# Attention and two expert layers on one core: column sums in two columns, a guard column for the combine sums, and a new plan of all queues

## The chip, the cores and the metric

The kernel runs on one core of one Trainium2 chip. The metric is the time of one execution on the device in microseconds (us); lower is better. The engines are PE (TensorE, matmuls), DVE (VectorE), ACT (ScalarE), POOL (GpSimd) and SP, which here only issues DMA transfers. Each engine works its own list of instructions in order and waits on semaphores for the others.

## What is computed

Three layers in a row. Blockwise causal attention over 8 batches, 8 heads, 576 positions of width 64; its output, 4608 rows of 512, goes through a soft mixture of experts (32 slots, 8 experts), and that through a bilinear layer.

```python
# attention, for each batch and head (blocks of 64 positions)
scores = scale * q @ k.T                     # masked where block_i < block_j
attn = exp(scores - max(scores, axis=-1))
attn = attn / (sum(attn, axis=-1) + 1e-09)
x = attn @ v
# soft mixture of experts on x (4608 x 512)
logits = x @ phi                             # 4608 x 32
d = exp(logits - logits.max(0)); d /= d.sum(0) + 1e-09     # dispatch: over all rows
slot_in = d.T @ x                            # 32 x 512, 4 slots per expert
slot_out[e] = relu(slot_in[e] @ w1[e]) @ w2[e]
c = exp(logits - logits.max(1)); c /= c.sum(1) + 1e-09     # combine: over 32 slots
x = c @ slot_out
# bilinear layer
out = ((x @ w1) * (x @ w2)) @ w3 @ w_out
```

## The kernel before

**Stages.** The attention stage takes the 64 heads as 32 pairs (n = 0 to 31), four pairs to a batch. Behind it come a short tail with the last batch's dispatch (`push_tail`), the experts together with the preparation of the weights of the last layer (`Rest.run`), and the output (`Rest.final`).

**One pair.** The steps have short names, which are those of the planner and of the methods `op_...`: `ld` and `ldv` load the pair (SP); `cast` (ACT, line 310) and `sub` (POOL, line 317) split it in a high and a low part; `M0` to `M3` (PE, line 329) make coarse scores, and `R0` to `R3` (DVE, line 333) reduce them to maxima in tile `bm`; `l2`, `mT`, `mc` and `mx` join the maxima, transpose them, copy them out and write them by four small transfers (lines 355 and 356, `shift<-mT`) into the tile X, from which the exact score matmuls `Q0` to `Q3` (PE, line 369) subtract them; `E0` to `E3` (ACT, line 377) are the exponentials, `P0`, `P1`, `P3` (POOL, line 387) sums of them, `V1` and `V0` (PE, lines 402 and 406) the products with v, `SU` (PE, line 418) and `sb` (DVE) the row sums. Scores of `M` and `Q` share three buffers in PSUM: a `Q` can start only when a reduction or an exponential has freed one.

**One batch**, while the next pairs run: `r` takes the reciprocals of the row sums (DVE, line 444), `rw` writes them to memory and `rd` reads them back spread over the partitions (SP, lines 449, 450 and 455), `sx0` to `sx3` multiply by them (POOL, line 459), `lg` makes the logits (PE, line 468) and `lgT` transposes them. The combine weights: `cm` maxima (line 487), `csub` (POOL, line 491), `cexp`, `csm` (DVE: sum in line 498, `+ 1e-9` in line 499, reciprocal in line 500), `cmul` (POOL, line 504), `cT` and its write. The dispatch weights: `LTm` (running column maxima, DVE), `LTe` (ACT, lines 544 to 548: two exponentials with their sums in `dac`, and `dal`, the factor by which older sums shrink when the maximum grows), `Ls` (DVE, lines 555 and 556: running column sums, the second part with weight 0.25, since the last 64 rows of a batch are held four times), `dn`, `xn0` to `xn4`, `S` and `SSu` (slot inputs).

**Fillers.** `b`-steps turn 64-bit weights of the last layer into f32 (a load and DVE and ACT steps, lines 823 to 838); `win` (line 848) loads the first expert windows, 2 MB each.

**What sets the order.** In the attention stage every engine's list is written out by the class `Plan`: each step has an engine, a guessed duration, a guessed time to landing (`lat`) for transfers, the steps it comes after, and a due time, n x PERIOD + OFF (plus EARLY for the first four pairs; for a batch step 4 x (batch + 1) x PERIOD + OFF). PE's list is the steps sorted by due time alone. The other engines take, at each moment of the planner's own clock, of the steps that become ready within LOOK the one with the least due time plus WAIT for each us it would have to be waited for. The planner's times only make the order; on the chip each engine goes by semaphores.

## Time and profile before

| | |
|---|---|
| three timed runs | 649.78, 649.06, 641.72 us; median 649.06 |
| profiled execution | 648.8 us, its span 647.0 us |
| granted PE clock over the span | 0.952 of full speed |
| PE busy | 597.0 us (92%) |
| PE weight loads | 433.3 us (67%) |
| DVE busy | 429.9 us (66%) |
| ACT busy | 323.1 us (50%) |
| POOL busy | 336.4 us (52%) |

The span runs from the first to the last instruction of the profiled execution; the device time has a little around it. PE's busy time is no measure of how dense its work is, since matmuls overlap in its pipeline; its idle time before an instruction, with what ended it, is the more telling figure. Granted clock 1.00 is 2.4 GHz and 0.50 is 1.2 GHz.

### The profile page before, as it was taken

How to read it: one execution, taken by the hardware profiler on the slowest of the kernel's cores; microseconds unless marked ns; L12 is line 12 of the kernel's file. 1: busy time of each engine (PE TensorE's matmuls, PEld its weight loads, DVE VectorE, ACT ScalarE, POOL GpSimd, SP SyncE). 2: the span in 40 equal slices, each digit the busy share in tenths (PEclk: the TensorE clock that was granted, in tenths of full speed). 3: DMA queues.
4: the chain of work that ended last, by engine and by line, in shares of the span. 5: the costliest groups of instructions: out<-in, count | busy, mean ns of one | idle time of the engine just before them, and what ended most of it. 6: DMA issues, size and time to landing. Idle time of an engine off the chain costs nothing.

```text
span 647.0 us, 13943 instructions
## 1 busy us (share of the span) xinstructions
PE 597.0 (92%) x5487; PEld 433.3 (67%) x5487; DVE 429.9 (66%) x714; ACT 323.1 (50%) x618; POOL 336.4 (52%) x245
## 2 busy tenths in 40 slices
PE   7999699989899899899897978879999979999997
PEld 4777577777676676677775745336655757888886
DVE  5568377786786786777782457899626998545550
ACT  4666277556564664665552622454324345444541
POOL 6879468858758578588464400344225223222220
PEclk8999699989989999999797997989999988999999
DMA  6356725526348239246145398999780314565642
GB/s 198 125 168 228 233 83 127 167 91 163 123 127 204 82 102 231 77 117 190 54 104 208 112 398 326 391 423 381 273 332 19 116 46 143 190 207 198 224 153 97
DMA packets 40441, 116.96 MB, mean 181 GB/s; under 512 B 6572, under 2 KB 16796, under 8 KB 38312
## 3 DMA queue, kind: packets, MB, share of 16 engines
q1 hardware_dynamic: 40196, 116.00, 54.0%
q8 instruction: 43, 0.70, 0.4%
q14 instruction: 22, 0.18, 0.1%
q10 hardware_dynamic: 180, 0.07, 0.0%
HBM read 105.75 MB, written 10.45 MB: 180 GB/s over the span
## 4 chain that ended last, share of the span: by engine, by line
PE 70%; DVE 12%; DMA 8%; issue 4%; ACT 3%; POOL 2%; SPq 0%; ACTq 0%; DVEq 0%; POOLq 0%
PE sc L369 16%; PE ops L1211 16%; PE pv L402 10%; PE wps L907 6%; PE sc L329 5%; DVE bm L333 4%; DMA shift<-mT 3%; PE pv L418 3%; DVE csm L499 2%; PE h L987 2%; DMA raw<-in_moe_w 2%; PE pv L468 1%; PE so L1014 1%; POOL wo L853 1%; PE ops L1213 1%
## 5 line engine op out<-in xcount | busy, mean ns | idle before, releaser
L333 DVE TENSOR_REDUCE bm<-sc 128x10 f32<-128x640 f32 (+2 forms) x128 | 122.6, 985 | 37.2 <-PE sc L329 36.8
L369 PE MATMUL sc<-set 64*128 64x320 f32 (+4 forms) x1152 | 124.3, 324 | 10.7 <-DVE bm L333 9.8
L369 PEld LDWEIGHTS sc<-set 64*128 64x128 f32 x1152 | 97.0, 201 | 22.8 <-DVE bm L333 14.2
L1211 PE MATMUL ops<-H,Ph 128*128 128x512 f32 x288 | 92.7, 402 | 3.0 <-ACT H L1115 2.5
L317 POOL TENSOR_TENSOR set<-raw,set 128x1152 fp32r<-128x1152 f32 x32 | 84.7, 2648 | 5.6 <-ACT set L310 2.4
L387 POOL TENSOR_TENSOR acc<-PTa,PTb 128x640 f32<-128x640 f32 x32 | 49.8, 1556 | 53.1 <-PE pv L418 44.8
L369 PE MATMUL sc<-shift 64*128 64x320 f32 (+4 forms) x384 | 64.5, 318 | 10.5 <-DMA shift<-mT 10.5
L1186 POOL TENSOR_TENSOR Pl<-rot,Ph 128x384 fp32r<-128x384 f32 x24 | 28.5, 1207 | 80.1 <-ACT Ph L1184 80.1
L1211 PEld LDWEIGHTS ops<-H,Ph 128*128 128x128 f32 x288 | 55.6, 193 | 17.3 <-ACT H L1115 2.9
L1211 PE MATMUL ops<-H,Pl 128*128 128x512 f32 x144 | 57.9, 402 | 0.0
L377 ACT ACTIVATE PTa<-sc 128x1024 f32<-128x1024 f32 x32 | 32.8, 1026 | 42.4 <-PE sc L369 37.9
L907 PE MATMUL wps<-wo,w 128*128 128x512 f32 x192 | 50.5, 405 | 2.7 <-POOL wo L853 1.7
L329 PE MATMUL sc<-set 64*128 64x320 f32 (+4 forms) x384 | 50.7, 338 | 0.8 <-ACT set L313 0.5
L369 PEld LDWEIGHTS sc<-shift 64*128 64x128 f32 x384 | 42.1, 202 | 13.3 <-DMA shift<-mT 12.8
L1214 ACT COPY o<-ops 128x512 f32<-128x512 f32 x36 | 21.1, 587 | 59.4 <-PE ops L1213 59.1
L387 POOL TENSOR_TENSOR acc<-acc,PTc 128x640 f32<-128x640 f32 x31 | 48.1, 1553 | 2.4
L907 PEld LDWEIGHTS wps<-wo,w 128*128 128x128 f32 x192 | 34.3, 188 | 20.1 <-issue 5.8
L411 ACT COPY xT<-pv 128x256 f32<-128x256 f32 (+1 forms) x64 | 25.5, 398 | 42.4 <-PE pv L406 32.0
L402 PE MATMUL pv<-PTc,v 128*64 128x256 f32 (+1 forms) x256 | 44.9, 430 | 1.0 <-ACT xT L411 1.0
L377 ACT ACTIVATE PTb<-sc 128x1024 f32<-128x1024 f32 x32 | 32.8, 1026 | 25.1 <-PE sc L369 23.4
L459 POOL TENSOR_TENSOR xT<-xT,shift 128x576 f32<-128x576 f32 x28 | 38.7, 1418 | 6.0 <-DMA shift<-rr 5.9
L377 ACT ACTIVATE PTc<-sc 128x640 f32<-128x640 f32 (+1 forms) x64 | 39.3, 650 | 3.7 <-PE sc L369 3.3
(246 smaller groups left out, 1161.7 us busy)
## 6 DMA issues: line engine op xcount, KB each, us to landing
win<-in_moe_w SPq DMA_DIRECT2D x16, 2048.0 KB
raw<-in_qk SPq DMA_DIRECT2D x32, 576.0 KB
v<-in_v SPq DMA_DIRECT2D x32, 320.0 KB
...
```

The costliest lines, as they stand in the source:

```text
L317: self.nc.gpsimd.tensor_tensor(lo, self.raw.pop(n), hi.bitcast(F32), op=ALU.subtract)
L329: self.nc.tensor.matmul(ps[:, h, o:o + kn], lhsT=qh[r, q0:q0 + 128], rhs=kh[r, k0:k0 + kn], start=True, stop=True)
L333: self.nc.vector.tensor_reduce(self.bmb[n % 2][:, :, o:o + m // 64], self.st.pop(("M", n, i))[:, :, 0:m].rearrange("p h (n k) -> p h n k", ...
L369: self.nc.tensor.matmul(ps[:, h, o0:o0 + w], lhsT=lt[r, k] if i < 3 else lt[r], rhs=rt[r, q0:q0 + w], start=i == 0, stop=i == 3)
L377: self.nc.scalar.activation(out=out, in_=ps[:, :, 0:sum(g[3] for g in self.UNITS[u])], func=AF.Exp, scale=SCALE)
L387: eng.tensor_tensor(acc[:, :, lo:hi], a, b, op=ALU.add)
L402: mm(ps[64 * h:64 * h + 64, q0 - lo:q1 - lo], lhsT=v[:, 128 * j + 64 * h:128 * j + 64 * h + 64], rhs=pt[:, h, o:o + q1 - q0], start=j == 0 ...
L411: self.nc.scalar.copy(self.xTb[b % 2][:, p, lo:hi], self.st.pop(("V", n, part))[:, 0:hi - lo])
L459: self.nc.gpsimd.tensor_tensor(x, x, self.rb[:, i], op=ALU.mult)
L907: nc.tensor.matmul(p, lhsT=a[:, o], rhs=b, start=c + i == 0, stop=c == 7 and i == 2)
L1186: eng.tensor_tensor(Pl[:, k], p, Ph[:, k].bitcast(F32), op=ALU.subtract)
L1211: nc.tensor.matmul(ps, lhsT=a[:, k, r], rhs=b[:, k], start=n == 0, stop=False)
```

## The change

Four things are edited. The column sums `Ls` are kept as two columns, one for each part: ACT multiplies the old ones by `dal` into a second row of `dac` (a new instruction of the first stage's `LTe`), one tensor_reduce on DVE adds the two rows, and the weight 0.25 is applied once, in the tail (`slot_sum`). The combine tile becomes a fixed tile of 33 columns, whose last column holds 1e-9, so that the reduction of line 498 adds the guard and line 499 goes; `cmul` now writes to a tile of its own. The planner's guesses change: 4.5 for 2.5 us to the landing of `rw`, 1.2 for 0.9 for `rd`, 0.52 for 0.9 for `csm`, and a little for `LTm`, `LTe` and `Ls`. The first window may be loaded after `Q0` of pair 6 instead of pair 4, and all due times and weights of the planner are other numbers.

```diff
--- before.py
+++ after.py
@@ -49,21 +49,21 @@
         nc.tensor.matmul(ps[:, 0:w], lhsT=keep["zeros"][:, 0:128], rhs=keep["zeros"][:, 0:w], start=True, stop=True)
 
 
-OFF = dict(ld=(145.85, -848.37, -88.58, 261.17), ldv=(773.65, 351.15, 347.6, 182.58),
-           cast=(-181.02, 301.68, 319.14, 419.66), sub=(278.96, -1281.51, 354.57, 216.03),
-           M0=(-68.45, -54.13, -78.59, -81.82), M1=(-72.52, -78.33, -71.42, -71.5),
-           M2=(-55.98, -86.85, -79.57, -63.38), M3=(-81.49, -85.42, -53.82, -73.3),
-           l2=(290.43, -440.49, -293.73, 999.35), mT=(-49.53, -43.88, -30.18, -33.86),
-           Q0=(-5.78, -20.61, -12.45, -4.41), Q1=(-2.38, -12.38, -4.76, 1.02), Q2=(1.6, -11.32, 8.14, 2.98),
-           Q3=(2.1, -9.94, 8.7, 1.71), P0=(-95.26, -384.06, -174.37, 299.52), P3=(104.53, 57.2, 67.07, 87.61),
-           V1=(42.63, 10.62, 11.84, 43.54), V0=(38.28, 27.09, 45.61, 18.15), SU=(23.27, 42.91, 38.78, 30.39),
-           r=254.78, sx0=162.82, sx1=-63.54, sx2=347.2, sx3=-32.45, lg=76.82, lgT=95.84, cm=652.17, cT=197.25,
-           LTm=16.4, dn=93.94, xn0=128.66, xn1=124.74, xn2=86.67, xn3=140.4, xn4=85.48, S=156, b=38.53)
-EARLY = dict(M=(-238.5, -160.13, -145.3, 8.44), m=(-163.57, -156.29, -130.1, 1.33), Q=(-156.25, -148.89, -5.6, -8.96))
-PERIOD = 32.899
-LOOK = dict(DVE=31.59, ACT=44.54, POOL=172.62, SP=79.34, PE=0)
-WAIT = dict(DVE=296.04, ACT=1322.25, POOL=154.39, SP=284.92, PE=0)
-BG0, BGS = 51.196, 1.727
+OFF = dict(ld=(192.13, -1003.31, 33.96, 308.08), ldv=(831.02, 395.8, 343.91, 147.85),
+           cast=(-124.13, 280.4, 312.63, 559.84), sub=(331.24, -1528.88, 431.86, 185.24),
+           M0=(-92.56, -65.33, -85.04, -97.01), M1=(-83.11, -82.9, -64.5, -69.87),
+           M2=(-58.52, -95.12, -80.33, -69.5), M3=(-92.88, -103.93, -50.22, -77.92),
+           l2=(332.47, -478.49, -253.38, 1132.37), mT=(-45.31, -39.92, -30.94, -41.28),
+           Q0=(-4.59, -16.6, -20.99, -9.6), Q1=(1.74, -11.46, -15.55, -5.94), Q2=(9.94, -9.79, -10.49, 6.36),
+           Q3=(-0.56, 0.89, 1.37, -2.61), P0=(37.42, -380.68, -165.87, 339.59), P3=(78.95, -43.79, 66.52, 137.55),
+           V1=(46.45, 9.48, 15.55, 44.48), V0=(39.73, 18.63, 52.08, 19.86), SU=(28.42, 39.49, 34.94, 34.16),
+           r=357.46, sx0=107.5, sx1=-193.83, sx2=217.14, sx3=11.51, lg=77.98, lgT=88.4, cm=705.09, cT=211.89,
+           LTm=13.08, dn=96.18, xn0=140.54, xn1=136.25, xn2=83.74, xn3=140.69, xn4=94.04, S=174.13, b=97.56)
+EARLY = dict(M=(-296.49, -199.51, -176.61, 5.24), m=(-238.54, -183.36, -167.65, -7.99), Q=(-174.47, -175.48, 3.44, -3.46))
+PERIOD = 35.238
+LOOK = dict(DVE=49.08, ACT=63.74, POOL=172.99, SP=85.93, PE=0)
+WAIT = dict(DVE=183.79, ACT=1358.44, POOL=120.38, SP=490.54, PE=0)
+BG0, BGS = 46.084, 1.836
 MX = ((.35, 1.22), (.29, 1.1), (.21, .83), (.24, .83))
 QK = ((1.2, 1.03), (1.11, 1.03), (.68, .71), (.54, .6))
 SHAPE = {"rows": .06, "cols": .08, "quarters": .28, "full": .07}
@@ -119,8 +119,8 @@
             at = lambda *names: [(x, b) for x in names]
             last = NP_B * b + NP_B - 1
             op("r", "DVE", 2.2, [("sb", last)] + old(b - 1, "rw"))
-            op("rw", "SP", 1.9, at("r") + old(b - 2, "rd"), lat=2.5, due="r", late=.1)
-            op("rd", "SP", .9, at("rw") + old(b - 1, *quarter("sx")), lat=8., due="r", late=.2)
+            op("rw", "SP", 1.9, at("r") + old(b - 2, "rd"), lat=4.5, due="r", late=.1)
+            op("rd", "SP", 1.2, at("rw") + old(b - 1, *quarter("sx")), lat=8., due="r", late=.2)
             for i in range(4):
                 op(f"sx{i}", "POOL", 1.45, at("rd") + [("c1", last - 3 + i), ("c0", last - 3 + i)])
             op("lg", "PE", 1.34, at(*quarter("sx")) + old(b - 1, "lgT", "LTe"), "pv", mode="quarters")
@@ -130,14 +130,14 @@
             op("cm", "DVE", .32, at("L4"))
             op("csub", "POOL", .46, at("cm") + old(b - 1, "cT"), due="cm", late=.1)
             op("cexp", "ACT", .34, at("csub"), due="cm", late=.2)
-            op("csm", "DVE", .9, at("cexp"), due="cm", late=.3)
+            op("csm", "DVE", .52, at("cexp"), due="cm", late=.3)
             op("cmul", "POOL", .46, at("csm"), due="cm", late=.4)
             op("cT", "PE", .32, at("cmul") + old(b - 1, "cTd"), "pv")
             op("cTc", "ACT", .46, at("cT"), free="cT", due="cT")
             op("cTd", "SP", 1.2, at("cTc"), lat=3, due="cT")
-            op("LTm", "DVE", .6, at("lgc"))
-            op("LTe", "ACT", 1., at("LTm") + old(b - 1, "dn", "SSu", "Ls"), due="LTm", late=.1)
-            op("Ls", "DVE", .3, at("LTe"), due="LTm", late=.2)
+            op("LTm", "DVE", .68, at("lgc"))
+            op("LTe", "ACT", 1.2, at("LTm") + old(b - 1, "dn", "SSu", "Ls"), due="LTm", late=.1)
+            op("Ls", "DVE", .16, at("LTe"), due="LTm", late=.2)
             op("dn", "PE", .3, at("LTe") + old(b - 1, "S"), "pv")
             op("dnc", "ACT", .35, at("dn"), free="dn", due="dn")
             for c in range(5):
@@ -156,7 +156,7 @@
             op("bm", "ACT", .67, at("bl") + old(j - 1, "b4"), due="b")
             op("b4", "DVE", .7, at("b3"), free="b1", due="b", late=.3)
         self.due = lambda t: t * PERIOD
-        for i, (t, after) in enumerate(((20, [("Q0", 4)]), (N - 3, [(q, n) for n in (N - 4, N - 3) for q in quarter("Q")]),
+        for i, (t, after) in enumerate(((20, [("Q0", 6)]), (N - 3, [(q, n) for n in (N - 4, N - 3) for q in quarter("Q")]),
                                         (N - 1, [(q, n) for n in (N - 2, N - 1) for q in quarter("Q")]),
                                         (N - 1, [(q, N - 1) for q in quarter("Q")]))):
             self.op(("win", i), "SP", .45, after, lat=10, due=t)
@@ -261,6 +261,7 @@
         self.xTb = [p.tile([128, NP_B, SP], F32, name=f"xT{i}") for i, p in enumerate((self.x_p, self.const))]
         self.Sb = self.const.tile([128, 384], F32, name="Sb")
         self.Lg = self.const.tile([128, 2, SP], F32, name="Lg")
+        self.C = self.const.tile([128, 5, 33], F32, name="Cb")
         self.dT = self.const.tile([128, 256], F32, name="dT")
         self.stage = self.xTb[1].rearrange("p a b -> p (a b)")
         self.xconst = self.stage[:, 640:640 + S]
@@ -271,6 +272,7 @@
         nc.vector.memset(self.ones, 0.0)
         for p in range(NP_B):
             nc.vector.memset(self.ones[:, p, p:p + 1], 1.0)
+        nc.gpsimd.memset(self.C[:, :, 32:33], EPS)
         nc.gpsimd.memset(self.Sb, 0.0)
         nc.gpsimd.memset(self.L[64:128, 4], 0.0)
         nc.gpsimd.memset(self.Lg[:, :, S:SP], 0.0)
@@ -487,21 +489,19 @@
         self.nc.vector.tensor_reduce(mx, self.L, axis=AX.X, op=ALU.max)
 
     def op_csub(self, b, _):
-        C = self.st["C"] = self.tl([128, 5, 32], "c")
-        self.nc.gpsimd.tensor_tensor(C, self.L, self.st["cm"].unsqueeze(2).to_broadcast([128, 5, 32]), op=ALU.subtract)
+        self.nc.gpsimd.tensor_tensor(self.C[:, :, 0:32], self.L, self.st["cm"].unsqueeze(2).to_broadcast([128, 5, 32]), op=ALU.subtract)
 
     def op_cexp(self, b, _):
-        self.nc.scalar.activation(out=self.st["C"], in_=self.st["C"], func=AF.Exp)
+        self.nc.scalar.activation(out=self.C[:, :, 0:32], in_=self.C[:, :, 0:32], func=AF.Exp)
 
     def op_csm(self, b, _):
         sm = self.st["csm"] = self.tl([128, 5], "csm")
-        self.nc.vector.tensor_reduce(sm, self.st["C"], axis=AX.X, op=ALU.add)
-        self.nc.vector.tensor_scalar(sm, sm, EPS, None, op0=ALU.add)
+        self.nc.vector.tensor_reduce(sm, self.C, axis=AX.X, op=ALU.add)
         self.nc.vector.reciprocal(sm, sm)
 
     def op_cmul(self, b, _):
-        C = self.st["C"]
-        self.nc.gpsimd.tensor_tensor(C, C, self.st["csm"].unsqueeze(2).to_broadcast([128, 5, 32]), op=ALU.mult)
+        C = self.st["C"] = self.tl([128, 5, 32], "c")
+        self.nc.gpsimd.tensor_tensor(C, self.C[:, :, 0:32], self.st["csm"].unsqueeze(2).to_broadcast([128, 5, 32]), op=ALU.mult)
 
     def op_cT(self, b, slot):
         ps, C = self.pv_b[slot], self.st["C"]
@@ -540,20 +540,18 @@
         self.nc.vector.tensor_scalar(ng, M, -1.0, None, op0=ALU.mult)
 
     def exps(self, b, t):
-        ac, ng, act = self.tl([128, 2], "dac"), self.st["ng"], self.nc.scalar.activation
-        act(out=self.dT[:, 0:128], in_=t[:, 0:128], func=AF.Exp, bias=ng, accum_out=ac[:, 0:1])
-        act(out=self.dT[:, 128:192], in_=t[:, 128:192], func=AF.Exp, bias=ng, accum_out=ac[:, 1:2])
+        ac, ng, act = self.tl([128, 2, 2], "dac"), self.st["ng"], self.nc.scalar.activation
+        act(out=self.dT[:, 0:128], in_=t[:, 0:128], func=AF.Exp, bias=ng, accum_out=ac[:, 0, 0:1])
+        act(out=self.dT[:, 128:192], in_=t[:, 128:192], func=AF.Exp, bias=ng, accum_out=ac[:, 0, 1:2])
         if b:
             al = self.st["al"] = self.tl([128, 1], "dal")
             act(out=al, in_=self.keep["M"][b % 2][:, 2:3], func=AF.Exp, bias=ng)
+            self.nc.scalar.mul(ac[:, 1], self.keep["Ls"], al)
         self.st["ac"] = ac
 
     def sums(self, b):
-        Ls, ac = self.keep["Ls"], self.st["ac"]
-        add = self.nc.vector.scalar_tensor_tensor
-        if b:
-            add(Ls, Ls, self.st["al"], ac[:, 0:1], op0=ALU.mult, op1=ALU.add)
-        add(Ls, ac[:, 1:2], 0.25, Ls if b else ac[:, 0:1], op0=ALU.mult, op1=ALU.add)
+        ac = self.st["ac"][:, 0:2 if b else 1]
+        self.nc.vector.tensor_reduce(self.keep["Ls"], ac.rearrange("p k c -> p c k"), axis=AX.X, op=ALU.add)
 
     def op_LTm(self, b, _):
         self.maxima(b, self.st["lgc"])
@@ -715,7 +713,9 @@
 
         def slot_sum():
             ps = pst("ML")
-            for i, t in enumerate((self.keep["M"][1 - b % 2][:, 2:3], self.keep["Ls"])):
+            Ls, tot = self.keep["Ls"], tl([128, 1], "tot")
+            nc.vector.scalar_tensor_tensor(tot, Ls[:, 1:2], 0.25, Ls[:, 0:1], op0=ALU.mult, op1=ALU.add)
+            for i, t in enumerate((self.keep["M"][1 - b % 2][:, 2:3], tot)):
                 nc.tensor.transpose(ps[0:1, 128 * i:128 * i + 128], t, ident)
             by_slot = lambda t: t.rearrange("p (g s) -> p s g", g=4)
             rows = lambda t: t.unsqueeze(1).to_broadcast([1, 4, 32])
@@ -1234,7 +1234,7 @@
     keep["sel32"] = kp.tile([128, 32], F32, name="sel32")
     keep["zeros"] = kp.tile([128, 512], mybir.dt.bfloat16, name="zeros")
     keep["M"] = [kp.tile([128, 3], F32, name=f"M{i}") for i in range(2)]
-    keep["Ls"] = kp.tile([128, 1], F32, name="Ls")
+    keep["Ls"] = kp.tile([128, 2], F32, name="Ls")
     keep["SS"] = kp.tile([128, 512], F32, name="SS")
     keep["L"], keep["C"] = (kp.tile([128, 5, 32], F32, name=f"last_{n}") for n in "LC")
     keep["siT"] = kp.tile([128, 4, 32], F32, name="siT")
```

## Rows read from the trace of the kernel before

**Rows 1.** Busy time by stretch: start:end, length, PE PEld DVE ACT POOL, PEclk

```profile
0.00:377.00 377.00, 350.04 (x4142) 262.17 (x4142) 257.15 (x440) 214.53 (x392) 263.09 (x184) 0.95 0.49 148
```

**Rows 2.** Waits: engine, line, waited for: us in total, times, longest

```profile
PEld sc L369 <- DVE bm L333: 14.2, 15, 2.2
...
PE sc L369 <- DMA shift<-mT: 10.5, 4, 5.3
...
PE sc L369 <- DVE bm L333: 9.8, 6, 2.0
```

**Rows 3.** Timeline of DVE: start us, us, line, operation [idle before <-what ended it]

```profile
219.43 0.75 DVE L555 SCALAR_TENSOR_TENSOR Ls<-Ls,dal,dac 128x1 f32<-128x1 f32 x1 [1.14 <-ACT dal L548]
220.21 2.55 DVE L556 SCALAR_TENSOR_TENSOR Ls<-dac,Ls 128x1 f32<-128x1 f32 x1
222.79 1.55 DVE L333 TENSOR_REDUCE bm<-sc 128x10 f32<-128x640 f32 x2
...
232.80 0.31 DVE L498 TENSOR_REDUCE csm<-c 128x5 f32<-128x160 f32 x1
233.14 2.41 DVE L499 TENSOR_SCALAR csm<-csm 128x5 f32<-128x5 f32 x1
...
237.37 2.15 DVE L444 RECIPROCAL rS<-Sb 128x320 f32<-128x320 f32 x1
```

**Rows 4.** Timeline of POOL, same batch and the next pairs

```profile
232.87 2.65 POOL L317 TENSOR_TENSOR set<-raw,set 128x1152 fp32r<-128x1152 f32 x1
...
237.26 1.56 POOL L387 TENSOR_TENSOR acc<-PTa,PTb 128x640 f32<-128x640 f32 x1 [0.88 <-ACT PTb L377]
...
252.79 5.52 POOL L459 TENSOR_TENSOR xT<-xT,shift 128x576 f32<-128x576 f32 x4 [0.74 <-DMA shift<-rr]
```

**Rows 5.** Timeline of PE, same batch

```profile
223.67 0.88 PE L369 MATMUL sc<-set 64*128 64x448 f32 x6 [1.97 <-DVE bm L333]
...
231.22 0.60 PE L527 MATMUL pv<-ident,xT 128*128 128x128 f32 x4
231.75 0.86 PE L369 MATMUL sc<-set 64*128 64x448 f32 x6
...
254.11 0.93 PE L369 MATMUL sc<-shift 64*128 64x448 f32 x2 [0.84 <-DMA shift<-mT]
...
260.41 1.50 PE L468 MATMUL pv<-xT,phi 128*32 128x128 f32 x64
```

**Rows 6.** Single lines: least/median/longest ns, first and last start us

```profile
L499 DVE TENSOR_SCALAR csm<-csm x7: 172/2416/2433, 98.5 to 372.9; 128x5 f32<-128x5 f32 x7
...
L556 DVE SCALAR_TENSOR_TENSOR Ls<-dac,Ls x7: 159/2549/2550, 128.9 to 391.3; 128x1 f32<-128x1 f32 x7
...
L548 ACT ACTIVATE dal<-M,dng x7: 278/279/289, 127.8 to 390.2; 128x1 f32<-128x1 f32 x7
```

**Rows 7.** Chain that ended last, in order of time: start us, us, what

```profile
188.22 2.43 DVE csm L499
...
277.91 2.41 DVE csm L499
...
324.16 2.44 DVE csm L499
```

**Rows 8.** Busy time by stretch again, two stretches of low PEclk (columns as in group 1)

```profile
72.40:83.10 10.70, 10.69 (x79) 8.31 (x83) 6.36 (x8) 5.80 (x9) 3.55 (x3) 0.50 0.39 144
...
311.80:318.60 6.80, 6.80 (x50) 6.06 (x50) 4.41 (x7) 2.78 (x5) 0.46 (x1) 0.50 0.25 80
```

**Rows 9.** Timeline of SP, transfers issued: start us, us of issue, line, operation

```profile
52.83 0.43 SPq L848 DMA_DIRECT2D win<-in_moe_w  x1
...
61.47 1.42 SPq L455 DMA_DIRECT2D shift<-rr  x2
...
241.41 1.40 SPq L455 DMA_DIRECT2D shift<-rr  x2
...
247.61 0.66 SPq L355 DMA_DIRECT2D shift<-mT  x1
```

## Prediction

> **What bounds the kernel now.** Five views were read, from coarse to fine. The stretches by stage come first: the attention stage is 377 of the 647.0 us of the span, and in it PE is busy 350.0, DVE 257.2, ACT 214.5 and POOL 263.1 us [rows 1]. PE runs one list in a fixed order, so a microsecond in which PE stands there is a microsecond of the end, and a microsecond of another engine counts only where PE ends up waiting for it. The diff touches this stage and a few instructions of the tail, so the question is where PE stands in it. The waits say: 9.8 us on the row maxima (line 333) and 10.5 us on the transfer that writes the maxima into X, `shift<-mT` [rows 2]. PE's timeline shows the first kind as a wait of 1.97 us at 223.67 [rows 5]; it comes back once in each of five batches, at 132.35, 177.23, 223.67, 268.44 and 311.63 (one row stands for the five; the sum of the five is nearly all of the 9.8).
>
> The maxima are only the messenger. On DVE the reduction that PE wants starts at 222.79, straight behind line 556, which takes 2.55 us for one column [rows 3]. Its median over seven is 2549 ns and its least 159 ns [rows 6]: the same instruction takes a sixteenth of that when nothing holds it. Line 499 is its twin: 2.41 us for five columns from 233.14, least 172 ns, and it ends at 235.55, when POOL's `sub` of 2.65 us that began at 232.87 ends too [rows 3, 4, 6]. So a DVE instruction with two operands in SBUF (556), or this form of tensor_scalar (499), waits for the POOL instruction that began before it. A tensor_reduce doesn't: line 498 took its 0.31 us from 232.80, across the start of that `sub` [rows 3, 4].
>
> **The change part by part.** Profiled execution: 648.8 us, span 647.0, so 1.8 us lie around it; the median of three is 649.06, and the sum is made against 648.8.
>
> *A, column sums.* Lines 555 and 556 go; one ACT multiplication and one tensor_reduce over four numbers come. In the list as it is, DVE gets ACT's last result at 219.43 and starts the wanted reduction at 222.79 [rows 3]. After: the multiplication costs what line 548, also one small ACT instruction, costs, 279 ns [rows 6], and the reduction at most the 0.31 us of line 498, which reads 160 columns. The wanted reduction then starts at 219.43 + 0.28 + 0.31 = 220.0, 2.8 us sooner; the wait that goes with it is 1.97. It goes wholly, with 0.8 us to spare, even if the list were not changed. Five times: **-9.7**. ACT's added 0.28 us lie inside DVE's wait and are in this reckoning; ACT is busy only 214.5 of 377 [rows 1]. The first batch's sums and those of the tail never stood on PE's path for long; the tail gains one DVE instruction for the final 0.25 weight and one on ACT: **+0.3**.
>
> *B, guard as a column.* Line 499 goes, seven times, six of them held. The reductions behind it start 2.4 us sooner, but PE had other work there: of 15 weight loads that waited for maxima, 14.2 us, five of at most 2.2 are those of A, so the other ten share at least 3.2 [rows 2]. Six of them follow a held 499; I take **-1.5**, bounds 0 and -3.2. The reduction over 33 columns for 32, the memset of the column and the separate output of `cmul` add instructions of a shape that is there already, on engines that are idle a third of the time: nothing, or 0.1 us a batch if POOL reads a pitch of 33 more slowly.
>
> Does the reciprocal of line 500 take over the wait of 499? The row that bears on it: line 444's reciprocal began at 237.37, 0.11 us after a POOL instruction of 1.56 us, and took 2.15 us, its time everywhere [rows 3, 4]. It was not held, so nothing moves. The Trainium skill (VectorE: DVE Perf Modes, What auto-detection actually checks) goes by operands: one source and a destination in SBUF of equal dimensions let an instruction take the second port, and line 500 is of that kind. By it 500 would be held as 499 was and B would give nothing, 631.5; the trace's row speaks against it, and the rule keeps a small chance below.
>
> *C, PE's clock.* After some of the waits of A the granted clock stood at 0.50 (1.2 GHz): 6.8 us from 311.8 [rows 8], and two like stretches of 3.4 us, from 134.3 and from 178.7 (one row stands for the three); none after the waits at 223.67 and 268.44. From one line 499 to the next is a batch: 188.22 to 233.14 is 44.92 us at full clock, and less its waits of 1.97 and, at 209.35, about 1.0 (like the 0.84 at 254.11) it is 41.9; 277.91 to 324.16 is 46.25, less 1.97 is 44.3, so 6.8 us of half clock cost 2.4, 0.35 a microsecond [rows 3, 5, 7]. For 13.6 us in all: **-4.4** (bounds 0 and -6.8, half of it all).
>
> *D, the first window.* The planner now lets the 2 MB load `win` go after pair 6 instead of pair 4. Before, it went at 52.83 in front of the writes of the reciprocals; the read behind these could go only at 61.47, 8.6 us later, straight into the transfers for pair 6 [rows 9]. This is the longest wait of PE for X, 5.3 us [rows 2], and it was followed by 10.7 us at half clock [rows 8], 3.7 by C's price: 9.0. In steady batches the read goes early enough (241.41, with the maxima of the pair at 247.61) that only 0.84 us are left at 254.11 [rows 5, 9]. The load is late next: it now stands somewhere ahead of pair 7's maxima and delays them if these come within its 8.6 us. I keep 2.5 for that: **-6.5**, bounds 0 and -9.0.
>
> *E, the new lists.* PE's list is its steps sorted by due time, so it can be worked out from the diff. Example: before, dn of batch 3 is due at 16 x 32.899 + 93.94 = 620.3, Q0 of pair 19 at 19 x 32.899 - 4.41 = 620.7, lgT at 622.2; after, lgT at 652.2, mT of pair 20 at 659.5, Q0 at 659.9, dn at 660.0. So lgT and the transposes move ahead of Q0 and dn behind it: more work of PE stands in front of the place of A. Ahead of Q0 of pairs 2, 6, 10 ... (the 0.84 us at 254.11) stands M0 of a later pair, 0.3 us more cover. The sorted list has 242 changes of the array's mode where it had 231. Four transposes from 231.22 take 0.60 us, 0.11 apart, and the first row-mode matmul follows the last of them by 0.20, at 231.75 [rows 5]: 0.09 for a change, **+1.0**. The lists of the other queues depend on the planner's clock and can't be read off. In it the writes of the reciprocals now last 2.0 us longer, so the read may be listed behind a load of the next pair. Waits that I can't place: **+2.0**, bounds 0 and, if each of seven batches got one more like the 0.84, +6.
>
> Sum: -9.7 + 0.3 - 1.5 - 4.4 - 6.5 + 1.0 + 2.0 = -18.8; 648.8 - 18.8 = **630.0 us**. All stages behind attention start from its end and move with it.
>
> **The rivals.** *The window load collides again* (with pair 7 as before with pair 6): D gives 0 and its reserve falls away, 636.5. For it: 2 MB are 2 MB; against it: the reciprocals' writes no longer queue behind it. *The read goes late*: SP lists it behind the next pair's load, it lands about 2 us later in each of seven batches and PE waits for X at the place of 254.11; with half clock behind some waits that is 2.4 a batch, +17, 647. For it: the planner's 4.5; against it: without 499 the reciprocals start up to 2.4 us sooner, which makes up for it. *Slower*: SP lists the read behind the maxima of the pair, past 250 instead of at 241.41 [rows 9], 8.7 us later. POOL's four multiplications by it ran from 252.79 for 5.5 us, to 258.3, and PE's list came to `lg`, which needs them, at 260.41 [rows 4, 5]. So from 2.1 us of delay on PE stands. The read would then find the queues emptier, so I count 4 of the remaining 6.6 us, in seven batches, and 1 each by the clock: +35, 665. Against it: a planner that reckons 8 us for the read sees this wait. *The reciprocal is held in place of 499*: line 500 starts where 499 did, in the first half microsecond of POOL's `sub`, waits for its end [rows 3, 4], and the 1.5 of B stay, 631.5; against it stands line 444, as said.
>
> **How the numbers follow.** Chances: forecast 0.57 (own range 622 to 637: C, D and E at their bounds), window again 0.15, late read 0.15, slower 0.08, reciprocal held 0.05. Time: 630.0. Range 620 to 648: below lies only C and D both in full, above it the slower rival and a part of the late read, together under 0.2. About 2%, 13 us, is what a measurement of this kernel can tell from no change. Faster by more, under 636.1: 0.52 of the forecast's 0.57, 0.07 of the window's, 0.04 of the last, 0.63. Slower by over 2%: 0.09. Within: 0.28.
>
> **What would show it.** A: no wait of PE near 2 us for line 333 in the batches; the sums' instruction on DVE at most 0.31 us long while POOL works. B: the reciprocal of the combine sums at its 0.19 us right behind the reduction, with POOL's `sub` still running. C: no half clock inside the batches between 90 and 330. D: no wait of 5 us for `shift<-mT` around 72, and batches of about 42 us from the first on. E: waits for `shift<-mT` of at most 1 us. The prediction is wrong if the batches stay near 45 us with the waits of A gone: then PE stands for X or for `lg` instead, and the read of the reciprocals on SP's timeline says which.

## The result, and the profile after

The changed kernel takes 621.42 us (median of 4 runs, 619.46 to 622.58) against 647.33 us; the ratio is 0.9608 with a 95% interval of 0.9536 to 0.9681, so it is faster by about 26 us. Timed again in a later comparison it gave 620.98 us and 0.9631 [0.9566, 0.9696]. The prediction was 630.0 us with a range of 620 to 648. The profiled execution is 620.63 us with a span of 618.8 us, 28.2 less than the span of before where the sum said 18.8 less.

In the code after, the names are the old ones and the lines move by two or so: the scores are lines 331 and 371, the row maxima 335, the reduction of the combine sums 499, its reciprocal 500, the column sums 554, POOL's `sub` 319 and `acc` 389.

The attention stage, busy time by stretch (length, PE, PEld, DVE, ACT, POOL, PEclk, DMA share, GB/s), which answers [rows 1]:

```profile
0.00:352.00 352.00, 336.86 (x4130) 253.51 (x4130) 225.08 (x426) 213.85 (x398) 262.40 (x185) 0.99 0.53 158
```

The stage ends 25 us sooner. DVE gives back 32 us of busy time, nearly all of it held time and not work: in the kernel before, the held runs of lines 499, 555 and 556 took some 29 us more than at their least. The granted clock rose from 0.95 to 0.99. PE's waits up to 345 us (us in total, times, longest), to set against [rows 2]:

```profile
PE sc L371 <- DMA shift<-mT: 3.0, 4, 1.6
PE pv L404 <- ACT xT L413: 2.0, 3, 1.1
...
PE sc L371 <- DVE bm L335: 0.9, 3, 0.3
```

The 9.8 us for the row maxima are 0.9, and the 10.5 us for the transfer into X are 3.0. The combine sums of a batch, to set against line 499 and POOL's `sub` in [rows 3, 4], in timelines of DVE and POOL of the kernel after:

```profile
218.13 0.32 DVE L499 TENSOR_REDUCE csm<-Cb 128x5 f32<-128x165 f32 x1
218.48 0.19 DVE L500 RECIPROCAL csm<-csm 128x5 f32<-128x5 f32 x1
218.73 1.96 DVE L335 TENSOR_REDUCE bm<-sc 128x16 f32<-128x1024 f32 x2
```

```profile
217.67 1.55 POOL L389 TENSOR_TENSOR acc<-acc,PTc 128x640 f32<-128x640 f32 x1 [0.28 <-ACT PTc L379]
```

The reduction and the reciprocal both ran inside a POOL instruction that began before them, neither was held, and the maxima follow 0.6 us after these sums began. In six of the seven places the two ran inside such an instruction and took their usual time; in the seventh POOL was idle. The column sums are short too, seven of their eight runs inside a POOL instruction (single line: least/median/longest ns):

```profile
L554 DVE TENSOR_REDUCE Ls<-dac x8: 146/146/158, 81.0 to 364.3; 128x2 f32<-128x4 f32 x7, 128x2 f32<-128x2 f32 x1
```

SP's transfers around the first window, to set against [rows 9]:

```profile
57.24 1.41 SPq L457 DMA_DIRECT2D shift<-rr  x2
62.74 0.68 SPq L357 DMA_DIRECT2D shift<-mT  x1
...
68.74 0.44 SPq L848 DMA_DIRECT2D win<-in_moe_w  x1
```

The read of the reciprocals (`shift<-rr`) goes 4 us sooner, and the window goes behind the maxima (`shift<-mT`) of its pair.

**A table for all kernels below.** All kernels but before and after are the runs of the next section. A batch is four pairs, and its length is read from ACT's timeline as the time between the first exponentials of two pairs that lie four apart. "Start" runs up to the first of them at pair 5, "five batches" are those after the first one, "last" runs from the last such mark to the end of the last exponential, "rest" from there to the end. Half clock is the time at 0.50 that begins between 90 and 320 us, where only the steady batches are. All in us, one profiled execution each.

| kernel | ratio to before, 95% | start | first batch | five batches | last | rest | half clock |
|---|---|---|---|---|---|---|---|
| before | 1 | 57.0 | 50.4 | 226.0 | 34.2 | 279.4 | 13.6 |
| after | 0.9608 [0.9536, 0.9681] | 58.4 | 42.8 | 210.8 | 30.8 | 275.9 | 0 |
| after, again | 0.9631 [0.9566, 0.9696] | 59.3 | 42.7 | 211.2 | 31.2 | 276.0 | 6.8 |
| edits alone | 0.9649 [0.9612, 0.9686] | 56.2 | 47.7 | 206.4 | 34.5 | 275.9 | 0 |
| plan alone | 0.9835 [0.9786, 0.9883] | 59.1 | 43.5 | 229.4 | 33.7 | 276.6 | 20.4 |
| column sums alone | 0.9758 [0.9706, 0.9810] | 57.0 | 48.5 | 212.0 | 35.4 | 276.2 | 0 |
| guard alone | 0.9957 [0.9923, 0.9991] | 57.0 | 48.0 | 223.5 | 35.6 | 278.5 | 17.0 |
| before, window late | 0.9949 [0.9909, 0.9989] | 56.2 | 43.7 | 228.2 | 34.5 | 278.7 | 17.0 |
| after, window early | 0.9678 [0.9619, 0.9736] | 59.8 | 47.2 | 208.5 | 31.4 | 276.7 | 0 |
| before, filled | 0.9853 [0.9799, 0.9906] | 56.3 | 47.8 | 216.4 | 36.1 | 277.2 | 0 |
| after, second window | 0.9610 [0.9559, 0.9662] | 59.3 | 42.7 | 206.7 | 27.5 | 275.3 | 0 |
| after, both tuned | 0.9524 [0.9482, 0.9566] | 59.1 | 43.1 | 207.5 | 27.3 | 274.0 | 0 |
| after, filler's square late | 0.9585 [0.9535, 0.9636] | 59.8 | 43.1 | 209.6 | 32.8 | 275.7 | 0 |
| edits, windows moved | 0.9481 [0.9427, 0.9535] | 56.9 | 45.4 | 205.2 | 29.7 | 278.5 | 0 |

Before against after, by column: +1.4, -7.6, -15.2, -3.4, -3.5, together -28.2 (with rounding). The profiled executions of "plan alone" (644.1 us) and of "edits, windows moved" (617.5) were the slowest of their runs and those of "filled" and of "second window" the fastest, so their rows count more for which waits stand in them than for their sums. The last but one column runs from 274.0 to 279.4 for kernels whose code there hardly differs, and it largely goes with the time at half clock behind the attention stage: 13.7 us in the kernel with 274.0, 20.5 in the kernel after, 24.6 in the kernel before, which has the largest value of all. By the price of experiment 4 these 4.1 us are 1.9 of the -3.5. No run takes the rest apart; I take it for the spread of single executions and not for the change.

The first batch has such a spread too. The filled kernel runs the same instructions as the kernel before until its first zeros, behind this batch, and its first batch is 47.8 us, not 50.4: the kernel before had 13.7 us of half clock behind its wait at the first window, the filled one 6.8 behind the same wait. So about 2.6 of the -7.6 are a longer half clock in the one profiled execution of before and no work of the change.

### The profile page after: what moved, and what is told of

Read it like the earlier page. It is cut to its first block, busy times and chain, and to the rows that moved or that the text cites. A ratio compares the mean times of both kernels' runs of the same rounds, so it can differ in the third digit from the quotient of the medians.

```text
span 618.8 us, 13858 instructions
## 1 busy us (share of the span) xinstructions
PE 581.2 (94%) x5475; PEld 423.2 (68%) x5475; DVE 396.7 (64%) x701; ACT 322.6 (52%) x625; POOL 337.8 (55%) x246
## 4 chain that ended last, share of the span: by engine, by line
PE 70%; DMA 13%; DVE 9%; POOL 3%; issue 3%; ACT 2%; SPq 0%; POOLq 0%; DVEq 0%; ACTq 0%
PE ops L1211 16%; PE sc L371 15%; PE pv L404 9%; DMA raw<-in_moe_w 7%; PE wps L907 7%; PE sc L331 4%; PE pv L420 4%; PE pv L527 3%; PE so L1014 2%; DVE bm L335 2%; DMA w3raw<-in_w3T 2%; PE h L987 2%; DMA raw<-in_qk 1%; PE ops L1213 1%; PE pv L470 1%
## 5 line engine op out<-in xcount | busy, mean ns | idle before, releaser
L371 PE MATMUL sc<-set 64*128 64x320 f32 (+4 forms) x1152 | 118.9, 313 | 1.5 <-DVE bm L335 0.9
L371 PEld LDWEIGHTS sc<-set 64*128 64x128 f32 x1152 | 92.3, 190 | 13.3 <-issue 6.3
L389 POOL TENSOR_TENSOR acc<-PTa,PTb 128x640 f32<-128x640 f32 x32 | 49.8, 1556 | 64.3 <-PE pv L420 43.5
L1186 POOL TENSOR_TENSOR Pl<-rot,Ph 128x384 fp32r<-128x384 f32 x24 | 30.6, 1296 | 76.8 <-ACT Ph L1184 76.8
L371 PE MATMUL sc<-shift 64*128 64x320 f32 (+4 forms) x384 | 61.6, 306 | 3.0 <-DMA shift<-mT 3.0
L379 ACT ACTIVATE PTc<-sc 128x512 f32<-128x512 f32 (+1 forms) x64 | 41.4, 649 | 24.2 <-PE sc L371 24.0
L907 PE MATMUL wps<-wo,w 128*128 128x512 f32 x192 | 50.4, 406 | 1.9 <-POOL wo L853 1.3
L331 PE MATMUL sc<-set 64*128 64x320 f32 (+4 forms) x384 | 48.2, 330 | 2.8 <-ACT set L312 1.9
L907 PEld LDWEIGHTS wps<-wo,w 128*128 128x128 f32 x192 | 34.5, 189 | 19.0 <-issue 5.4
L371 PEld LDWEIGHTS sc<-shift 64*128 64x128 f32 x384 | 39.2, 190 | 5.9 <-DMA shift<-mT 5.3
L379 ACT ACTIVATE PTb<-sc 128x1024 f32<-128x1024 f32 x32 | 32.8, 1026 | 17.1 <-PE sc L371 13.5
```

Of the source, the lines that this page charges most:

```text
L331: self.nc.tensor.matmul(ps[:, h, o:o + kn], lhsT=qh[r, q0:q0 + 128], rhs=kh[r, k0:k0 + kn], start=True, stop=True)
L371: self.nc.tensor.matmul(ps[:, h, o0:o0 + w], lhsT=lt[r, k] if i < 3 else lt[r], rhs=rt[r, q0:q0 + w], start=i == 0, stop=i == 3)
L379: self.nc.scalar.activation(out=out, in_=ps[:, :, 0:sum(g[3] for g in self.UNITS[u])], func=AF.Exp, scale=SCALE)
L389: eng.tensor_tensor(acc[:, :, lo:hi], a, b, op=ALU.add)
L907: nc.tensor.matmul(p, lhsT=a[:, o], rhs=b, start=c + i == 0, stop=c == 7 and i == 2)
L1186: eng.tensor_tensor(Pl[:, k], p, Ph[:, k].bitcast(F32), op=ALU.subtract)
```

## The experiments

**1. Which half of the change carries it.** The first kernel has all new operations and the planner's numbers of before; the second has the operations of before and all the new numbers (due times, `LOOK`, `WAIT`, guessed durations, the place of the first window).

```diff
 edits alone = after with
-PERIOD = 35.238
+PERIOD = 32.899
 ...
```

> The changed operations (guard column, two column sums) with the plan of before. My theory: each of the five waits of about 2 us for bm behind the held sums goes, and the clock then stays whole inside the batches, so the batches after the first shorten by some 2 to 2.6 us each: about 634 (630 to 637). The X wait of about 5 us near 72 us and the half clock behind it stay. Rival, that the edits pay only with lists made for them: 643 or more. Rival, that the edits are the whole gain and the lists none: 622.

> The operations of before in the order of the new plan. My theory: the new order removes the X wait near 72 us and the half clock behind it (7 to 9 us) and the same kind of wait at the last window (3 to 6 us), and pays for some held sums, so 634 to 639, with waits of PE for bm left. Rival, that the lists are the whole gain: 622. Rival, that the order, made for shorter sums, collides with the held ones: 645 or more.

Measured: 623.29 and 636.5 us beside 645.77. The edits alone are 22.5 us of the change, a good deal more than the 15 to 16 that I gave them, and the time lies outside the 630 to 637 that was expected. The new lists bring what is left, some 2 us, inside the intervals. Alone the plan brings 9 us, as expected (634 to 639). So the two halves do not add up: alone they are 3.5% and 1.65%, together 3.7 to 3.9%. Waits of PE between 60 and 340 us, first edits alone, then plan alone:

```profile
PE sc L371 <- DMA shift<-mT: 9.9, 3, 4.9
PE pv L404 <- ACT xT L413: 0.4, 1, 0.4
```

```profile
PE pv L344 <- DVE m L341: 7.3, 5, 1.5
PE pv L402 <- ACT xT L411: 5.9, 5, 1.9
PE sc L369 <- DVE bm L333: 1.3, 3, 0.7
```

With the edits, the old list has no wait in the batches left but for X: 4.9 us at the first window, 4.2 us at the second, 0.8 us once between. With the plan and the held instructions the waits for the maxima (9.8 before) became 1.3, since other work stands in front of them now, and two others came in their place, five times each and 13.2 us together. One is the same held instruction with another victim: DVE's maxima of the maxima (`m`, line 341) come to stand behind the column sum of 2.54 us, and PE's transposes wait for them (timelines of DVE and of PE):

```profile
126.92 2.54 DVE L556 SCALAR_TENSOR_TENSOR Ls<-dac,Ls 128x1 f32<-128x1 f32 x1
129.41 0.07 DVE L339 MEMSET bm<- 64x4 f32 x2
129.52 0.25 DVE L341 TENSOR_REDUCE m<-bm 128x10 f32<-128x90 f32 x1
```

```profile
129.91 0.27 PE L344 MATMUL pv<-ident,m 128*10 128x128 f32 x1 [1.47 <-DVE m L341]
```

The other, for copies of ACT, comes from the new list itself (experiment 7). So in this profile the new order gains nothing at the held instructions that it does not lose elsewhere; its gain is at the first window. Of the edits my theory named the price wrongly, and its rival (the edits are the whole gain) is nearer: 622 against 623.3.

The table shows why the lists bring so little: against the edits alone the kernel after has -4.9 in the first batch and -3.7 at the end, both at a window, and pays +2.2 at the start and +4.4 in the five batches.

**2. Which edit.** Each of the two edits alone, on the list of before.

```diff
 column sums alone
 ...
-        add(Ls, ac[:, 1:2], 0.25, Ls if b else ac[:, 0:1], op0=ALU.mult, op1=ALU.add)
+        self.nc.vector.tensor_reduce(self.keep["Ls"], ac.rearrange("p k c -> p c k"), axis=AX.X, op=ALU.add)
 ...
 guard alone
 ...
-        self.nc.vector.tensor_reduce(sm, self.st["C"], axis=AX.X, op=ALU.add)
-        self.nc.vector.tensor_scalar(sm, sm, EPS, None, op0=ALU.add)
+        self.nc.vector.tensor_reduce(sm, self.C, axis=AX.X, op=ALU.add)
 ...
```

> Only the column sums of the maxima's row sums are changed (one tensor_reduce into two columns, joined at the end), with the plan of before. My theory: this edit carries the five waits for bm, 9.7 us, and up to 4.4 us of half clock: about 635 (633 to 639). Rival, that the guard edit carries half of it: 641 or more. Rival, that another instruction takes the held place and the wait stays: 646 or more.

> Only the guard is changed to a constant column (the held tensor_scalar goes away), with the plan of before. My theory: DVE's 2.4 us hold is mostly beside work that PE does not wait for, so 0 to -3, about 646. Rival, that the hold is what makes bm late: 638 or less. Rival, that the reciprocal is then held in its place: 647, no change, with a reciprocal of over 1 us in the trace.

Measured: 630.46 (-15.3) and 643.95 us (by its ratio -2.8, between -0.6 and -5.0). The first gains 4 us more than my figure, which lies just outside its interval (626.8 to 633.5); in its five batches it gains 14.0, where A and C said 14.1. The second is as I expected while the other holds are still there. Waits of PE between 60 and 340 us, guard alone and then column sums alone:

```profile
PE sc L371 <- DVE bm L335: 9.7, 5, 2.0
PE sc L371 <- DMA shift<-mT: 4.9, 1, 4.9
```

```profile
PE sc L369 <- DMA shift<-mT: 11.8, 6, 5.1
```

So the guard edit does not touch the five waits for the maxima, and the column sums take all of them.

On top of the column sums the guard edit shortens the five batches by 5.6 us (212.0 to 206.4). PE works the same list in these two kernels, so the starts of the same instructions, counted from the mark of their batch, show where. 2.0 us of it, 0.4 in every batch, come right behind the held line 499: the reduction that frees a buffer of scores stands behind it on DVE, and PE's next scores start when that reduction ends (column sums alone: DVE, then PE; then PE with the edits alone):

```profile
138.88 2.40 DVE L499 TENSOR_SCALAR csm<-csm 128x5 f32<-128x5 f32 x1
141.32 0.19 DVE L500 RECIPROCAL csm<-csm 128x5 f32<-128x5 f32 x1
141.42 1.05 DVE L333 TENSOR_REDUCE bm<-sc 128x14 f32<-128x896 f32 x1
```

```profile
142.09 0.31 PE L369 MATMUL sc<-shift 64*128 64x320 f32 x2
142.53 0.62 PE L369 MATMUL sc<-set 64*128 64x256 f32 x6
```

```profile
139.56 0.31 PE L371 MATMUL sc<-shift 64*128 64x320 f32 x2
139.71 0.52 PE L371 MATMUL sc<-set 64*128 64x256 f32 x6
```

Most of these waits are too short to stand in the sums above. 3.2 us come at X, in three of the five batches (0.9, 1.4, 0.9). That is an effect that I had not seen: with the guard edit alone the small waits for X inside the batches are gone, and without it, with the column sums alone, four of them stand there (11.8 us in all, six times, with the two at the windows). Guard alone gains at the same two places against the kernel before, 2.0 and 2.1 us, and gives 1.6 back where it has 17.0 us at half clock for 13.6. A way to X shows on SP. In the steady batches of every kernel with the old list and without the guard edit (before, column sums, filled, window late) the read of the reciprocals is issued 6.2 us before the maxima of the pair (5.8 in the last); with the edit (guard alone, edits alone, edits with windows moved) it is 6.8 us (6.7 in the last), as the held line 499 stood in front of the large reciprocal on DVE that SP's writes wait for. One batch, column sums alone and then edits alone:

```profile
188.53 1.39 SPq L455 DMA_DIRECT2D shift<-rr  x2
194.70 0.66 SPq L355 DMA_DIRECT2D shift<-mT  x1
```

```profile
184.63 1.38 SPq L457 DMA_DIRECT2D shift<-rr  x2
...
191.40 0.66 SPq L357 DMA_DIRECT2D shift<-mT  x1
```

PE comes to X 5.5 us after the issue of the maxima. Over the five steady batches of each kernel it then waited in 10 of 20 at 6.2 us of distance and in 1 of 15 at 6.8. That the read, when it is close, is what delays the maxima is argued from these counts and not shown by a run that moves the read alone, and distance alone does not decide: the filled kernel had 6.2 and no wait in five, and the seven profiles with the new lists have 7.1 to 7.3 and yet wait 0.2 to 0.8 us in 9 of 35 such batches, 3 of them in the kernel after. In the new list a filler's load of 512 KB is issued between the read and the maxima, 1.4 us in front of them (SP, kernel after); no run moves it either.

```profile
227.79 1.37 SPq L457 DMA_DIRECT2D shift<-rr  x2
...
233.57 0.42 SPq L823 DMA_DIRECT2D raw<-in_moe_w  x1
234.94 0.67 SPq L357 DMA_DIRECT2D shift<-mT  x1
```

**3. The first window.** One entry of SP's list is moved: in the kernel before behind `ldv.7`, in the kernel after back in front of the writes of the reciprocals.

```diff
+            steps = Plan(self.nb).order()
+            late = next(x for x in steps if x[0] == ('win', 0))
+            steps.remove(late)
+            steps.insert(1 + next(i for i, x in enumerate(steps) if x[0] == ('ldv', 7)), late)
```

> The kernel of before with one SP entry moved: the first window of the gates is issued behind the load ldv.7, three entries later. My theory: the X wait of about 5 us near 72 us and the half clock behind it go, 7 to 9 us: about 639.5 (637 to 642). Rival, that the collision moves on to the next pair of maxima: 645 to 648 with a wait of like size one pair later. Rival, that the half clock there has another cause: about 642, only the wait gone.

> The changed kernel with one SP entry moved back: the first window is issued in front of rw.0, as before the change. My theory: the X wait and the half clock near 72 us come back, 6 to 9 us: about 629 (627 to 631). Rival, that the other new places of the start carry the gain of the first batch: 622, no change.

Measured: 643.97 us, where 639.5 (637 to 642) was expected, and 626.49, a little under the 627 to 631 expected; ratios 0.9949 and 0.9678 (0.9608 and 0.9631 for the kernel after). The wait of 5 us goes with the entry (0.6 us are left of it) and comes back with it (3.4 us, and 6.8 us of half clock from 73.5). In the first batch that is -6.7 in the one and +4.4 in the other. Of the 6.7 some 2.6 are the longer half clock in that one execution of before: against the filled kernel, guard alone and column sums alone, all with the window early, the first batch is 4.1 to 4.8 shorter. So the window is worth some 4 us. The time fell by some 3 (0.7 to 5.9 by the interval): the five batches after it grew by 2.2 us in the profiled execution, with 17.0 us at half clock where the kernel before had 13.6, in two of them 6.8 us at a time behind waits for the maxima that had cost no clock before. That this gives a part back is argued from one execution each and not shown by a run.

**4. Is the clock a cost of its own.** In the kernel before, 14 matmuls of zeros stand in front of the place where PE waits for the maxima.

```diff
+        if b:
+            warm(self.nc, self.keep, ps[:, 256:512], 14, 256)
```

> The kernel of before with 14 matmuls of zeros (128 x 256, bf16) behind dn's transposes in each batch but the first, into columns of PSUM that nothing reads, so that PE works during the wait for bm. About 14 x 0.11 = 1.5 us of PE work, so the wait for bm shows as a shorter one, and no time is saved in itself. My theory: if the wait of 2 us is what makes the clock fall, the half clock of 3.4 us near 134 and 179 us and part of that near 312 us goes, and the time falls by 0 to 4.4: about 645. Rival, that the clock inside the batches has another cause: 647 to 652, with the half clock at the same places.

Measured: 637.15 us, 0.9853 [0.9799, 0.9906]: 10 us faster with more work in it, where 645 was expected. Timeline of PE around the place, filled kernel:

```profile
170.04 1.69 PE L49 MATMUL pv<-zeros 128*128 128x256 bf16 x14
172.19 0.87 PE L369 MATMUL sc<-set 64*128 64x448 f32 x6 [0.46 <-DVE bm L333]
```

The zeros take 1.69 us and 0.46 us of the wait is left, so the wait of 2 us is all still there as time; all that can have gone is what comes behind it. Between 100 and 310 us (columns as in the first fence) the kernel before and the filled one:

```profile
100.00:310.00 210.00, 199.28 (x2505) 150.25 (x2497) 157.47 (x258) 127.45 (x242) 159.40 (x106) 0.98 0.50 138
```

```profile
100.00:310.00 210.00, 207.15 (x2631) 157.52 (x2629) 163.62 (x269) 131.59 (x249) 161.82 (x107) 1.00 0.50 140
```

No half clock is left in the steady batches. What one stretch costs can be read from the same instructions at either clock: in the kernel before, from the scores behind the wait to the first matmul with `ones`, and the same in the kernel with the edits alone:

```profile
177.23 0.88 PE L369 MATMUL sc<-set 64*128 64x448 f32 x6 [1.97 <-DVE bm L333]
...
182.79 0.40 PE L418 MATMUL pv<-PTc,ones 128*32 128x256 f32 x1
```

```profile
167.87 0.88 PE L371 MATMUL sc<-set 64*128 64x448 f32 x6
...
171.90 0.40 PE L420 MATMUL pv<-PTc,ones 128*32 128x256 f32 x1
```

5.56 us against 4.03: 1.5 us for 3.4 us at half clock, 0.45 a microsecond, where the prediction took 0.35. The Trainium skill (TensorE: Matmul & The Clock Gate, HAM oscillation) reckons half of the time at the lower clock as lost; these rows come close to it. For 13.6 us that is 6.1. The filled kernel's five batches gained 9.6. Set side by side with the kernel before, instruction by instruction as in experiment 2, 6.1 of it come at the three places of the half clock (1.5, 1.5 and 3.1) and the other 3.5 at X, nearly all in the two batches in which the kernel before waits there (1.02 and 0.84 us, 1.6 and 1.5 with what follows). Why the filled kernel did not wait for X in its batches no run shows. So the clock is a cost of its own, about 6 of the 10 us.

**5. The last window, and the start.** In the kernel after the same kind of collision stands at the second window (PE's timeline):

```profile
324.61 0.84 PE L371 MATMUL sc<-shift 64*128 64x448 f32 x2 [1.60 <-DMA shift<-mT]
```

```diff
 second window (in words)
+            (the entry ('win', 1) of SP's list moves behind ('mx', 30))
 both tuned: the same, and
-EARLY = dict(..., Q=(-174.47, -175.48, 3.44, -3.46))
+EARLY = dict(..., Q=(-190.0, -175.48, 3.44, -3.46))
```

> The changed kernel with the second window's entry on SP moved behind the last maxima's load (mx.30). My theory: the last collision of the changed kernel, PE's wait of 1.8 us for the transposed maxima near 324.6 us and the half clock of 3.4 us behind it, goes: 618 to 620 against 621.4. Rival, that the experts' gates then come late: 621 or more, with a wait of PE for the window's product.

> The changed kernel with the second window behind mx.30, and the first quarter of Q due 15.5 us earlier at the start, so that it stands ahead of M0.2 in PE's order. My theory: the start's wait at 14.2 us (2.2 us, with 6.8 us of half clock against 3.4 before the change) was the 1.4 us that the first pair comes later than before, and it goes: 617 to 619. Rival, that the start is paced by the loads: the same time as with the second window alone.

Measured: 618.79 and 613.73 us, ratios 0.9610 and 0.9524. In both profiles the wait is gone and the last stretch is 3.3 to 3.5 us shorter. In the times it shows in one of them only: the ratio of the first is that of the kernel after, with runs from 613.4 to 624.84. That one is inconclusive, and the second lies under the 617 to 619 that was expected. The start did not do what I expected: in "both tuned" the half clock there is 3.4 us in place of 6.8, but the mark at pair 5 stands at 59.1 as without it, so something else paces it, perhaps the loads, as the rival said. The intervals of the two kernels just touch; whether this one is really the faster, and why, stays open.

**6. Both gains without the cost.** If the new lists gain only at the two windows and cost in the batches, the old list with the edits and three moved entries should beat the kernel after. The kernel after runs beside it.

```diff
 edits, windows moved = edits alone with
+            for key, behind in ((('win', 0), ('ldv', 7)), (('win', 1), ('mx', 30)), (('bl', 14), ('mx', 30))):
+                (the entry key of SP's list moves behind the entry behind)
```

> The changed kernel itself, unchanged, beside the next kernel on the same chip: 621 (619 to 623), ratio to before about 0.961. If the new plan is worth nothing on top of the edits it stands level with the run of the edits alone (623.3).

> The changed operations with the plan of before, and three SP entries moved: the first window behind ldv.7, the second window and the filler load bl.14 behind the last maxima's load mx.30. My theory: what the new plan gains lies at the two windows alone (4.9 us in the first batch, 6.0 us in the last batch and pairs, by the profiles of the changed kernel and of the edits alone), and what it costs lies in the middle batches (42.7 us each against 41.0); so this kernel has both gains without that cost: 623.3 - 4.9 - 6.0 = 612 (610 to 616), below the changed kernel. Rival, that the gains at the windows need the new order of the other engines too: 619 to 624, level with it or above. Rival, that the second window then comes late for the experts' gates: 616 to 620, with a wait for it behind the last pair.

Measured: 620.98 and 611.45 us, ratios 0.9631 [0.9566, 0.9696] and 0.9481 [0.9427, 0.9535]; 612 was expected of the second. It has the lowest median and ratio here, 9.5 us below the changed kernel on the same chip. But "both tuned", the new lists with both windows out of the way and one entry at the start moved, comes to 0.9524 [0.9482, 0.9566], and the two intervals overlap. So the moved windows are shown to pay (0.9649 to 0.9481 on the old list); that the old list is the better one in the batches is not shown by the times, only by the table's rows (205.2 and 206.4 against 206.7 to 211.2). Between 100 and 310 us PE did not wait once and was busy 209.54 of 210 us:

```profile
100.00:310.00 210.00, 209.54 (x2700) 159.99 (x2700) 148.18 (x274) 138.69 (x265) 168.57 (x113) 1.00 0.51 143
```

In the kernel after it was busy 206.01:

```profile
100.00:310.00 210.00, 206.01 (x2619) 155.92 (x2617) 148.58 (x275) 135.49 (x261) 164.77 (x109) 1.00 0.52 144
```

**7. What the new lists cost in the batches.** In the kernel after, ACT comes to the square of a filler block (`m<-raw`) before the block's load has landed, with the copy `xT` that PE needs queued behind it (timeline of ACT, then of PE's victim in the waits above, 1.1 us):

```profile
198.54 0.67 ACT L836 ACTIVATE m<-raw 128x512 bf16<-128x512 f32 x1 [3.48 <-DMA raw<-in_moe_w]
199.11 0.41 ACT L413 COPY xT<-pv 128x320 f32<-128x320 f32 x1
```

Between 100 and 310 us it stands there 13.4 us in four places; with the edits alone, on the old list, ACT has no such wait. With the plan alone it has it too, 16.8 us in four places. Five of these squares are moved behind the copy:

```diff
+            for key, behind in ((('bm', 1), ('c1', 4)), (('bm', 4), ('c1', 8)), (('bm', 7), ('c1', 12)), ...):
+                (the entry key of ACT's list moves behind the entry behind)
```

> The changed kernel with five entries on ACT moved: in the lists of the new plan ACT comes to the square of a filler block (m<-raw, bm of blocks 1, 4, 7, 10, 13) before the load of that block has landed and idles 3.5 us on it, with the copy xT that PE needs queued behind it. Here each stands behind that copy. My theory: this is what the new lists cost in the steady batches, so ACT's idle time in front of that copy and the waits of PE for xT (2.0 us, longest 1.1) go and the five batches come from 211 to 207 to 209, the time to 618 to 620. Rival, that the filler's steps on DVE, now later, hold the maxima instead: 621 or more, with waits of PE for bm or m. Rival, that the cost lies in the order of PE: 211 as before, with the waits gone.

Measured: 621.9 us, 0.9585 [0.9535, 0.9636], not to be told from the kernel after, where 618 to 620 was expected; 209.6 us in the five batches. PE's waits for `xT` are gone between 100 and 310 us, and waits for the maxima are there, 3.1 us in two places. The first rival names it: DVE, too, has the filler's steps ahead of what PE wants, and it stands for the same load longer than ACT did.

```profile
157.42 0.69 DVE L834 TENSOR_SCALAR pv<-raw 128x512 int32<-128x512 int32 x1 [5.57 <-DMA raw<-in_moe_w]
...
158.76 1.95 DVE L335 TENSOR_REDUCE bm<-sc 128x10 f32<-128x640 f32 x2
```

```profile
159.63 0.56 PE L371 MATMUL sc<-set 64*128 64x320 f32 x4 [1.84 <-DVE bm L335]
```

So moving the steps of one engine only moved the wait; in both kernels what is waited for is the same load that lands late. That an earlier load would end these waits is likely but not shown: a kernel with that load issued earlier was not run.

## Why the prediction was right, and where not

The way and the order of size were right: A, C and D are there, and the edits remove the waits that were named. The time, 621.42, lies near the lower end of the range of 620 to 648 and just under the 622 to 637 of the forecast itself. That it is inside is partly luck: the lower end was reckoned from C and D in full, and what brought the time there was B, the second window and the part behind attention. Two figures of the working are off: 13.6 us at 0.35 a microsecond are 4.8 and not 4.4, and with C, D and E at their upper bounds the forecast's range ends near 645 and not at 637.

**A, column sums: right, with its size.** The waits for the maxima fell from 9.8 to 0.9 us, the sums take 0.146 us of DVE and the maxima follow at once. Set side by side, instruction by instruction, the kernel before and the one with the column sums differ by 1.8 us at each of the five places, 9.1 in all for the 9.7. That the edit alone gains 14.0 in the five batches, where A and C together said 14.1, is partly luck: C brings 6.1 and not 4.4, and the waits for X, which stand in four batches where before there were two, take 1.1 back.

**B, guard: the step that was mis-sized most.** -1.5 was taken, -3.2 was the bound. On top of the column sums the edit is worth 5.6 us in the five batches (212.0 to 206.4), 7 by the ratios 0.9758 and 0.9649, which leave 3 to 11. The prediction looked for its price only among the waits for the maxima, and there it is 2.0 us in the five batches, well inside the bounds. The larger part, 3.2, came at X: the waits for X in [rows 2], which I let stand in E, go on the old list when the guard edit is made. The likely way is that the held instruction also stands in front of the large reciprocal, so the read on SP goes later, closer to the maxima; that way is argued and not shown (experiment 2). What is queued behind a held instruction was followed one step, to the next reductions, and not to the transfers that come after them.

**The reciprocal in place of 499: no.** It ran 0.19 us in all seven places, in six of them inside POOL's `acc`; the held line 499 of the kernel with the plan alone, a tensor_scalar, was held by that same `acc` (0.77 us). The rule of the Trainium skill (VectorE: DVE Perf Modes, What auto-detection actually checks) taken by operands alone would have had it wait; the trace agrees with line 444 and not with that reading.

**C, the clock: right in kind, a little small in price.** No half clock stands between 90 and 320 us in the kernel after (6.8 us in its second profile), and the filled kernel shows that it is a cost by itself: 0.45 a microsecond, 6.1 us for 13.6, for the 4.4 of the sum.

**D, the first window: right in kind, a little large.** -6.5 was said and the first batch is 7.6 us shorter, but 2.6 of that are the longer half clock in the one profiled execution of before: edits alone, guard alone, column sums alone and the filled kernel, all with the wait still at 4.8 to 5.1 us, have 6.8 us of half clock there and 47.7 to 48.5 us. The moved window is worth 4.1 to 4.8 on the list of before (experiment 3), 4.9 between edits alone and the kernel after, and 2.3 in "edits, windows moved", where 3.4 us of half clock come later in that batch. No new collision came with pair 7: the window goes behind the maxima of pair 6, and PE has no wait for X there.

**E, the new lists: the reserve was spent.** +3.0 was taken. In the five batches the six kernels with the new lists and the edits take 206.7 to 211.2 (mean 209.1), the two with the old list 206.4 and 205.2: about +3.3. Five of the six have the same lists there and still spread over 4.5 us, so the size is rough. The changes of mode can hardly be it (31 in a steady batch for 30). The waits that were left are not at a late read of the reciprocals, which goes sooner than before, but at a filler's load (experiment 7) and, 0.2 to 0.6 us at a time, at X with such a load in front of it (experiment 2). The start pays another 2.2 against the edits alone.

**What no step had.** First, the second window: -3.4 in the last stretch. Before, SP issued the second window and a filler's load in front of the maxima of pair 30, and the wait behind it (3.3 us, what is left of the 10.5 in [rows 2] when the three placed ones are taken out) was in the row and in no step. In the kernel after 1.6 us of it are left (experiment 5), so the sign under E, waits of at most 1 us, failed at this one place. Second, -3.8 of tail and output against the sum's +0.3, of which the half clock there is some 1.9 and no run explains the rest. Third, the start, +1.4. With B short by 4.1 that is 9.9 less, about the 9.4 us between the sum and the span.

**The rivals.** The window did not collide again, the read did not go late (the largest wait for X between 100 and 310 us is 0.6 us), PE waits nowhere for the multiplications in front of `lg`, and the reciprocal was not held.
